# Two tiles' attention ahead of the weights, and a third tile in float32 products, in a fused attention and feed-forward kernel

## Chip, cores and metric

The kernel runs on one core of one Trainium2 chip. The metric is the device time of one execution in microseconds (us), and a lower time is better. The engines are called by their names in the profile: PE is the tensor engine, DVE the vector engine, ACT the scalar engine, POOL the GpSimd engine, and SP the engine that issues the transfers.

## What is computed

The reference is a decaying linear attention over 4 sequences of 768 positions with 8 heads of 64 features, followed by a two-layer feed-forward network with a squared ReLU:

```
for b in range(nb):
    intra = np.einsum('bhic,bhjc->bhij', qb, kb) * Dmask[None]
    intra = np.einsum('bhij,bhjd->bhid', intra, vb)
    inter = np.einsum('bhid,bhde->bhie', qb * lam_pow[None], kv_state)
    out[:, :, sl] = intra + inter
    kv_state = lam_block * kv_state + np.einsum('bhsd,bhse->bhde', kb * rev_pow, vb)
x = out as 3072 rows of 512
h = np.maximum(x @ w_in, 0.0)          # w_in 512 x 2048
return (h * h @ w_out)                 # w_out 2048 x 512
```

## The kernel before, in words

The 3072 rows are cut into 24 chunks of 128 positions, one for each sequence b and each of its six chunks c. Three chunks make a tile of 384 rows, so there are eight tiles (`TILES`). Tile 0 holds the chunks (0,0), (1,0), (2,0); tile 1 holds (3,0), (0,1), (0,2); tile 2 holds (0,3), (0,4), (0,5); every later tile holds further chunks of sequences 1 to 3. A chunk with c above 0 needs the state that the chunk before it in its sequence leaves behind.

**Attention.** Each chunk is worked in two units of four heads (q = 0 and 1), so a tile has six units. There are two forms. `unit_plain` multiplies float32 operands: scores (L312), the masked scores on DVE (L315), scaled values `vd` (L318), the state's update (L330, then `us` L340 and `diag` or `hold` L345 on DVE), the products with the old state and with the values (L357 and L360), and then `xr`, `xh` and `xl` (L363, L366, L367). `unit_split` cuts its operands into a high and a low part and multiplies these (L421, L441, L463, L464), which costs more work on ACT and DVE. The first `N_PLAIN` tiles take the plain form, the others the split form. The buffers of the plain form and of the weights (`pnt`, `diag0`, `diag1`, `st`, `m`) share their memory with those of the split form (`pkt`, `ab` and others): the split form starts when the last plain unit and the last weight are done.

**Weights.** The feed-forward network has 16 steps f. Each needs two halves of weights, 128 x 512 of the first layer (`wih`, `wil`) and 128 x 512 of the second (`woh`, `wol`). The weights arrive as 64-bit words. For each half ACT takes an absolute value (L271), DVE does four operations that turn the word into a float32 (L272, L274, L276, L278), ACT rounds the high part (L280), and DVE subtracts it for the low part (L281). There are three buffers `st` for arriving halves. After step 15 has been loaded the weights stay.

**Feed-forward step.** For one tile and one f, PE makes 12 products with 384 columns (L498) into `h`; ACT and DVE make `gh` and `gl` from it (for tiles 0 and 1 the ReLU, the square and the rounding are on ACT, later the square is repeated on DVE, L518); PE then makes six products with 512 columns (L504, L505) and three more (L507). Tiles have six PSUM banks and two `h` banks to share with the attention.

**Order.** All operations are listed with an engine, an expected length and a key. `Plan.order` goes through expected time and on each engine takes, among the operations that could start next, the one with the smallest key. The result is one fixed order for each engine; engines then wait only for data and buffers. The constants `FIRST`, `SLOW_STEP`, `LAG`, `SECOND` and `STEP` set the keys: tile 0's steps begin at `FIRST`, those of tile 1 sixteen steps later. Where `Plan.order` expects PE to be idle before `FILL_END`, it puts in a product of zeros (`filler`, L233), which writes into the second `h` bank. At the very start the table for the decay is turned by PE (`turned`, L245) after POOL has made the powers.

Of the kernel before, what the change touches and what calls it, by code (L numbers as in the profile page):

```python
# [19 lines left out]
P = 128  # L20
C = 128
# [18 lines left out]
TILES = [CHUNKS[j:j + NT] for j in range(0, B * NC_, NT)]  # L40
N_PLAIN = 2
PLAIN = [bc for t in TILES[:N_PLAIN] for bc in t]
# [18 lines left out]
class Plan:  # L61
# [16 lines left out]
    def order(self, pe_slow, fill):  # L78
# [9 lines left out]
        slots = {k: [(0.0, i) for i in range(n)] for k, n in self.slots.items()}  # L88
        done, early = [], sum(o.early is True for o in self.ops)
        while any(ready.values()):  # L90
# [25 lines left out]
            if o.eng == "PE" and t < fill:  # L116

                while free["PE"] + FILL < t:
                    done.append(Op("PE", FILL, 0, self.filler, [], [], [], 0, None))
                    done[-1].start, done[-1].end = free["PE"], free["PE"] + FILL  # L120
                    free["PE"] += FILL
            dur = o.dur * (2.0 if o.eng == "PE" and t < pe_slow else 1.0)
# [13 lines left out]
            for d in out.get(id(o), ()):  # L136
                need[id(d)] -= 1
                if not need[id(d)]:
                    ready[d.eng].append(d)
        assert sum(o.fn is not self.filler for o in done) == len(self.ops), "operations need each other"  # L140
        return done
# [12 lines left out]

FIRST, SLOW_STEP, LAG, SECOND, STEP, PE_SLOW, FILL_END, FILL = 18.0, 6.5, 16, 5.0, 4.8, 8.0, 24.0, 0.43

# [4 lines left out]
def kernel(ctx: ExitStack, tc: tile.TileContext, pn, pk, lamx, w, out):  # L161
# [69 lines left out]

    def filler():
        nc.tensor.matmul(tiles["h"][-1][:, 0:2 * P], zero[:, 0:P], zero[:, P:3 * P], start=True, stop=True)  # L233

# [8 lines left out]
    def turned():  # L243
# [6 lines left out]
        [o_pow], [wb], early=True)  # L250
    o = plan.op("PE", 0.9, 3, turned, [o], [wb, rps], early=True)
    o_rdec = plan.op("DVE", 0.6, 3, lambda: nc.vector.tensor_tensor(
# [42 lines left out]

    def unit_plain(b, c, q, x, col, key):

# [3 lines left out]
        def add(eng, dur, dk, fn, deps, bufs, name=None):  # L301
            o = plan.op(eng, dur, key + dk, fn, deps, bufs, early=True)
            return in_turn(name, o) if name else o

        load = add("SP", 1.7, -8, lambda: nc.sync.dma_start(out=at(t), in_=pn[PLAIN.index((b, c)), q]), [o_start], [t], "load")
        so = []
        for h in range(2):
            sc = Buf("bank")

            def scores(h=h, sc=sc):  # L310
                for n in range(2):
                    nc.tensor.matmul(at(sc)[:, n * C:n * C + C], at(t)[half(h), 0, n], at(t)[half(h), 1, n], start=True, stop=True)  # L312

            o = add("PE", 0.33, 0, scores, [load], [t, sc], f"sc{h}")
            so.append(add("DVE", 0.36, 0, lambda h=h, sc=sc: nc.vector.tensor_tensor(  # L315
                out=at(s1).rearrange("p (n h) i -> p n h i", h=2)[:, :, h], in0=at(sc)[:, 0:2 * C].rearrange("p (n i) -> p n i", n=2),
                in1=mask.unsqueeze(1).broadcast_to([P, 2, C]), op=ALU.mult), [o], [sc, s1], f"s1{h}"))
# [43 lines left out]

        o = add("PE", 1.25 if old else 0.8, 0.2, values, so + [o_vd] + ([old[1]] if old else []), [y, t, vd, s1] + ([old[0]] if old else []), "y")
        o = add("DVE", 0.35, 0.2, lambda: nc.vector.tensor_tensor(  # L363
# [7 lines left out]
    def unit_split(b, c, q, x, col, key, span):  # L371
# [83 lines left out]
        for h in range(2):  # L455
# [12 lines left out]

            o = add("PE", 0.48, 2, values, [ov2, op2, os2], [vv, pp, y, ss, ab], f"y{h}")
            o1 = add("ACT", 0.32, 2, lambda h=h, part=part: nc.scalar.copy(at(z)[:, h], part(1)), [o], [y, z], f"z{h}")  # L470
# [15 lines left out]

    last_mm = {}

    def ffn(ti, f, x, ready, wo, os_, key):
# [19 lines left out]
        o1 = plan.op("PE", 2.09, key, mm1, list(ready) + list(wo[0]), [x, h], [last_mm.get((ti, 1))])  # L509
        last_mm[ti, 1] = o1  # L510

        orr = plan.op("ACT", 0.45, key, lambda: nc.scalar.activation(at(g), at(h)[:, 0:N], AF.Relu), [o1], [h, g])  # L512
        if ti < N_PLAIN:
            og = plan.op("ACT", 0.45, key, lambda: nc.scalar.activation(at(g), at(g), AF.Square), [orr], [g])
            ogh = plan.op("ACT", 0.47, key, lambda: nc.scalar.copy(at(gh), at(g)), [og], [g, gh])  # L515
        else:
            ogh = plan.op("ACT", 0.47, key, lambda: nc.scalar.activation(at(gh), at(g), AF.Square), [orr], [g, gh])  # L517
            og = plan.op("DVE", 0.48, key, lambda: nc.vector.tensor_tensor(out=at(g), in0=at(g), in1=at(g), op=ALU.mult), [orr, ogh], [g])  # L518
# [34 lines left out]
    for ti, cs in enumerate(TILES):  # L553
# [3 lines left out]
        for j, (b, c) in enumerate(cs):  # L557
            for q in range(NQ):
                i = j * NQ + q
                if ti == 0:  # L560
                    ready += unit_plain(b, c, q, x, j * C, i * 1.5)
                elif ti < N_PLAIN:
                    ready += unit_plain(b, c, q, x, j * C, FIRST + 2 + i * SECOND)
                else:

                    f0 = 0.5 if ti > N_PLAIN else 2.0
                    ready += unit_split(b, c, q, x, j * C, begin[ti - 1] + (f0 + i / n * (13 - f0)) * per[ti - 1], 4.0)
# [59 lines left out]
```

## Time and profile before

| quantity | value |
|---|---|
| median of 3 runs | 660.7 us (660.07 to 660.84) |
| profiled execution | 660.94 us, its span 659.2 us |
| mean granted PE clock, share of full speed | 0.991 |
| PE busy | 641.5 us (97%), 3576 products |
| PE weight loads (PEld) | 576.3 us (87%) |
| DVE busy | 510.0 us (77%) |
| ACT busy | 364.7 us (55%) |
| POOL busy | 5.5 us (1%) |
| transfers | 58.30 MB, mean 88 GB/s |

The span is the time from the first to the last instruction of the profiled execution; 1.74 us of its time lie around the span. An engine is busy while one of its instructions runs. PE's products overlap, so a busy PE is not always a PE at its full rate: a product of 512 columns shows some 0.4 us, but the next one starts after 0.23 us. Where a duration counts below, it is therefore taken from one start to the next.

### The profile page before, as it was taken

The numbers are of one execution on the slowest core, as the hardware profiler recorded it, in microseconds if no ns is written. First come the engines' busy times: TensorE is split into PE (matmuls) and PEld (weight loads), VectorE is DVE, ScalarE is ACT, GpSimd is POOL, SyncE is SP. The second block draws the span as 40 slices with busy tenths as digits, with TensorE's granted clock in tenths as the row PEclk, the third lists the DMA queues.
The fourth block names the chain that finished last, engine by engine and source line by source line (L and its number), as shares of the span: only waits on it lengthen the run. The fifth ranks groups of instructions, "written<-read, shape, count | busy, mean of one in ns | idle before, by whom it ended". The sixth has DMA issues, their size and how long they took to land.

```text
span 659.2 us, 9528 instructions
## 1 busy us (share of the span) xinstructions
PE 641.5 (97%) x3576; PEld 576.3 (87%) x3576; DVE 510.0 (77%) x1150; ACT 364.7 (55%) x805; POOL 5.5 (1%) x15
## 2 busy tenths in 40 slices
PE   8869899999999999999999999999999999999997
PEld 7757798999989989899989999899998998999996
DVE  5979999978996889579995899848996698842222
ACT  2444576668884567456663565636665556532222
POOL 2000000000000000000000000000000000000000
PEclk9979899999999999999999999999999999999999
DMA  7733445622223112014111212220220221000001
GB/s 269 270 135 114 161 158 176 221 96 96 96 93 100 47 51 96 33 66 144 48 49 57 87 56 96 89 81 17 95 97 1 96 96 49 1 32 17 1 0 49
DMA packets 15167, 58.30 MB, mean 88 GB/s; under 512 B 1808, under 2 KB 1808, under 8 KB 15120
## 3 DMA queue, kind: packets, MB, share of 16 engines
q1 hardware_dynamic: 15120, 57.68, 25.5%
q8 instruction: 28, 0.46, 0.3%
q14 instruction: 19, 0.16, 0.1%
HBM read 51.39 MB, written 6.29 MB: 87 GB/s over the span
## 4 chain that ended last, share of the span: by engine, by line
PE 76%; DVE 19%; ACT 3%; DMA 1%; issue 1%; SPq 0%; ACTq 0%
PE h L498 33%; PE bank L507 12%; PE bank L504 11%; PE bank L505 11%; PE bank L464 2%; PE bank L463 2%; PE bank L421 2%; DVE gl L519 1%; DVE xr L476 1%; PE bank L441 1%; DVE ab L407 1%; DVE s L429 1%; PE h L233 1%; DVE ka L409 1%; DVE g L518 1%; DVE pp L433 1%
## 5 line engine op out<-in xcount | busy, mean ns | idle before, releaser
L504 PE MATMUL bank<-woh,gh 128*128 128x512 f32 x384 | 153.0, 398 | 2.1 <-ACT gh L515 2.1
L505 PE MATMUL bank<-wol,gh 128*128 128x512 f32 x384 | 152.2, 396 | 0.0
L512 ACT ACTIVATE g<-h 128x384 f32<-128x384 f32 x128 | 62.8, 491 | 132.1 <-PE h L498 131.5
L498 PE MATMUL h<-xh,wih 128*128 128x384 f32 x512 | 111.1, 339 | 5.1 <-ACT wih L280 5.1
L507 PE MATMUL bank<-woh,gl 128*128 128x512 f32 x384 | 112.8, 402 | 0.7
L518 DVE TENSOR_TENSOR g<-g 128x384 f32<-128x384 f32 x96 | 53.5, 557 | 77.3 <-ACT gh L517 76.8
L498 PE MATMUL h<-xh,wil 128*128 128x384 f32 x512 | 110.4, 338 | 0.0
L498 PE MATMUL h<-xl,wih 128*128 128x384 f32 x512 | 110.1, 337 | 0.0
L498 PEld LDWEIGHTS h<-xh,wih 128*128 128x128 f32 x512 | 90.6, 190 | 9.6 <-ACT wih L280 5.3
L498 PEld LDWEIGHTS h<-xh,wil 128*128 128x128 f32 x512 | 91.2, 189 | 0.0
L498 PEld LDWEIGHTS h<-xl,wih 128*128 128x128 f32 x512 | 91.0, 189 | 0.0
L507 PEld LDWEIGHTS bank<-woh,gl 128*128 128x128 f32 x384 | 70.1, 189 | 19.2 <-DVE gl L519 4.8
L504 PEld LDWEIGHTS bank<-woh,gh 128*128 128x128 f32 x384 | 72.5, 189 | 16.0 <-ACT gh L515 2.7
L505 PEld LDWEIGHTS bank<-wol,gh 128*128 128x128 f32 x384 | 72.7, 189 | 13.3
L519 DVE TENSOR_TENSOR gl<-g,gh 128x384 fp32r<-128x384 f32 x128 | 71.0, 556 | 8.7 <-ACT gh L515 4.5
L517 ACT ACTIVATE gh<-g 128x384 fp32r<-128x384 f32 x96 | 50.4, 525 | 2.5
L470 ACT COPY z<-bank 128x256 f32<-128x256 f32 x72 | 26.7, 371 | 38.2 <-PE bank L464 35.6
L471 DVE TENSOR_TENSOR z<-bank,z 128x256 f32<-128x256 f32 x72 | 30.0, 423 | 20.4 <-ACT z L470 18.8
L464 PE MATMUL bank<-pp,vv 128*128 128x256 f32 x144 | 35.8, 281 | 0.0
L463 PE MATMUL bank<-ab,ss 128*128 128x256 f32 x144 | 35.7, 281 | 0.0
L428 ACT COPY s<-bank 128x256 f32<-128x256 f32 x72 | 24.4, 373 | 17.7 <-PE bank L421 17.4
L476 DVE TENSOR_TENSOR xr<-z,zl 64x256 f32<-64x256 f32 x72 | 30.0, 417 | 2.5 <-ACT zl L472 1.0
(79 smaller groups left out, 801.3 us busy)
## 6 DMA issues: line engine op xcount, KB each, us to landing
pkt<-pk SPq DMA_DIRECT2D x36, 768.0 KB, 4.4
st<-w SPq DMA_DIRECT2D x32, 512.0 KB, 3.4
pnt<-pn SPq DMA_DIRECT2D x12, 512.0 KB, 4.7
out<-ob SPq DMA_DIRECT2D x23, 256.0 KB, 2.1
out<-z SPq DMA_DIRECT2D x1, 256.0 KB, 2.0
lam<-lamx SPq DMA_DIRECT2D x1, 6.0 KB, 1.6
```

The lines of the kernel that those rows point to most:

```text
L463: nc.tensor.matmul(y4[:, n], at(ss)[:, n, h].rearrange("p t d -> p (t d)"), at(ab)[:, i], start=n == 0, stop=False, skip_group_check=True)
L464: nc.tensor.matmul(y4[:, n], at(vv)[:, i].rearrange("p t d -> p (t d)"), at(pp)[:, i], start=False, stop=True, skip_group_check=True)
L471: zo.append(add("DVE", 0.36, 2, lambda h=h, part=part: nc.vector.tensor_tensor(out=at(z)[:, h], in0=part(0), in1=at(z)[:, h], op=ALU.add), ...
L476: nc.vector.tensor_tensor(out=at(xr)[half(h)], in0=at(z)[0:64, h], in1=at(zl)[:, h], op=ALU.add)
L498: nc.tensor.matmul(at(h)[:, 0:N], wt[:, cc, :], xt[:, cc, :], start=k == 0, stop=k == 3 * NCC - 1)
L504: nc.tensor.matmul(at(os_[j]), at(gh)[:, sl], woh[f], start=f == 0, stop=False)
L505: nc.tensor.matmul(at(os_[j]), at(gh)[:, sl], wol[f], start=False, stop=False)
L507: nc.tensor.matmul(at(os_[j]), at(gl)[:, sl], woh[f], start=False, stop=f == NF - 1)
L512: orr = plan.op("ACT", 0.45, key, lambda: nc.scalar.activation(at(g), at(h)[:, 0:N], AF.Relu), [o1], [h, g])
L517: ogh = plan.op("ACT", 0.47, key, lambda: nc.scalar.activation(at(gh), at(g), AF.Square), [orr], [g, gh])
L518: og = plan.op("DVE", 0.48, key, lambda: nc.vector.tensor_tensor(out=at(g), in0=at(g), in1=at(g), op=ALU.mult), [orr, ogh], [g])
L519: ogl = plan.op("DVE", 0.48, key, lambda: nc.vector.tensor_tensor(out=at(gl), in0=at(g), in1=at(gh), op=ALU.subtract), [og, ogh], [g, gh, gl])
```

## The change

The change sets `N_PLAIN` to 3, so tile 2 takes the plain form, and 30 split units remain of 36. The units of tile 2 are loaded no earlier than step 12 of tile 0 (`BEHIND`), and their values product takes the buffer of its tile's `x`. Tile 1's attention has keys from `BEGIN2` = 9 in steps of 1.5 instead of 20 in steps of 5, so it stands right behind that of tile 0 and ahead of nearly all weights; the order of the feed-forward steps of tile 0 and 1 follows from what can then start. The zero products write into a free bank instead of the second `h` bank, count as longer while PE is expected to be slow, may go on until 45, and stand at the start only until the first load is expected; the turning of the decay table waits for the first scores. ACT keeps the square for tiles 0 and 1 only (`ti < 2`, formerly `ti < N_PLAIN`), so tile 2's feed-forward steps are as before.

```
-N_PLAIN = 2
+N_PLAIN = 3
...
-                while free["PE"] + FILL < t:
-                    done.append(Op("PE", FILL, 0, self.filler, [], [], [], 0, None))
-                    done[-1].start, done[-1].end = free["PE"], free["PE"] + FILL
-                    free["PE"] += FILL
+                while free["PE"] + (long := FILL * (2.0 if free["PE"] < pe_slow else 1.0)) < t:
+                    bank = min(slots["bank"], default=(t, 0))
+                    if bank[0] > free["PE"]:
+                        break
+                    done.append(Op("PE", long, 0, lambda i=bank[1]: self.filler(i), [], [], [], 0, None))
+                    done[-1].start, done[-1].end = free["PE"], free["PE"] + long
+                    free["PE"] += long
+                    filled += 1
...
-FIRST, SLOW_STEP, LAG, SECOND, STEP, PE_SLOW, FILL_END, FILL = 18.0, 6.5, 16, 5.0, 4.8, 8.0, 24.0, 0.43
+FIRST, SLOW_STEP, LAG, BEGIN2, SECOND, STEP, PE_SLOW, FILL_END, FILL = 18.0, 6.5, 16, 9.0, 1.5, 4.8, 7.0, 45.0, 0.43
+
+BEHIND = 12
...
-    def filler():
-        nc.tensor.matmul(tiles["h"][-1][:, 0:2 * P], zero[:, 0:P], zero[:, P:3 * P], start=True, stop=True)
+    def filler(i):
+        nc.tensor.matmul(tiles["bank"][i][:, 0:2 * P], zero[:, 0:P], zero[:, P:3 * P], start=True, stop=True)
...
-        load = add("SP", 1.7, -8, lambda: nc.sync.dma_start(out=at(t), in_=pn[PLAIN.index((b, c)), q]), [o_start], [t], "load")
+        load = add("SP", 1.7, -8, lambda: nc.sync.dma_start(out=at(t), in_=pn[PLAIN.index((b, c)), q]), [o_start, behind], [t], "load")
...
+            if (b, c, q) == (0, 0, 0):
+                o_turned.after.append(o)
...
-        if ti < N_PLAIN:
+        if ti < 2:
...
+                elif ti == 1:
+                    ready += unit_plain(b, c, q, x, j * C, BEGIN2 + i * SECOND)
                 elif ti < N_PLAIN:
-                    ready += unit_plain(b, c, q, x, j * C, FIRST + 2 + i * SECOND)
+                    ready += unit_plain(b, c, q, x, j * C, begin[ti - 1] + (1 + i / n * 11) * per[ti - 1], steps[0, BEHIND])
```

What this does to the order shows at three places. In the rows, a name is that of the buffer written, then those read; lines of the changed kernel are six to eight higher (L233 is L239, L245 is L251, L312 is L318, L330 is L338, L360 is L368, L498 is L506, L504, L505 and L507 are L512, L513 and L515, L281 is L287).

The first place is PE at the very start, before:

```order
L233 MATMUL h_68<-ob_79 128x256 x11
L245 MATMUL bank_61<-g_77,m_184 128x128 x4
L312 MATMUL bank_62<-pnt_173 128x128 x2
L312 MATMUL bank_63<-pnt_173 128x128 x2
L312 MATMUL bank_64<-pnt_174 128x128 x2
L312 MATMUL bank_65<-pnt_174 128x128 x2
L330 MATMUL bank_66<-vd_90,pnt_173 64x64 x4
L360 MATMUL bank_61<-s_0_88,vd_90 64x128 x4
```

And now:

```order
L239 MATMUL bank_61<-ob_79 128x256 x5
L318 MATMUL bank_61<-pnt_173 128x128 x2
L318 MATMUL bank_62<-pnt_173 128x128 x2
L338 MATMUL bank_63<-vd_90,pnt_173 64x64 x4
L368 MATMUL bank_64<-s_0_88,vd_90 64x128 x4
L318 MATMUL bank_65<-pnt_174 128x128 x2
L318 MATMUL bank_66<-pnt_174 128x128 x2
L251 MATMUL bank_61<-g_77,m_184 128x128 x4
L368 MATMUL bank_62<-s_1_89,vd_91 64x128 x4
```

Six zero products have gone, and the first unit's scores, update and values product and the second unit's scores stand ahead of the turned table.

The second place is PE at its first feed-forward steps (`xh_95` is tile 0, `xh_97` is tile 1, `wih_106` is step 0, `wih_107` step 1), before:

```order
L498 MATMUL h_67<-xh_95,wih_106 128x384 x4
L498 MATMUL h_67<-xl_96,wih_106 128x384 x4
L498 MATMUL h_67<-xh_95,wil_122 128x384 x4
L330 MATMUL bank_63<-vd_90,pnt_175 64x64 x4
L312 MATMUL bank_61<-pnt_173 128x128 x2
L360 MATMUL bank_62<-s_0_88,vd_90 64x128 x4
L330 MATMUL bank_63<-vd_91,pnt_176 64x64 x4
L498 MATMUL h_68<-xh_95,wih_107 128x384 x4
L498 MATMUL h_68<-xl_96,wih_107 128x384 x4
L498 MATMUL h_68<-xh_95,wil_123 128x384 x4
L312 MATMUL bank_62<-pnt_174 128x128 x2
L498 MATMUL h_67<-xh_95,wih_108 128x384 x4
```

And now, from the last state update of tile 1 on:

```order
L338 MATMUL bank_64<-vd_91,pnt_176 64x64 x4
L239 MATMUL bank_62<-ob_79 128x256 x4
L506 MATMUL h_68<-xh_97,wih_106 128x384 x4
L506 MATMUL h_68<-xl_98,wih_106 128x384 x4
L506 MATMUL h_68<-xh_97,wil_122 128x384 x4
L515 MATMUL bank_61<-woh_138,gl_72 128x512
L515 MATMUL bank_65<-woh_138,gl_72 128x512
L515 MATMUL bank_66<-woh_138,gl_72 128x512
L506 MATMUL h_67<-xh_95,wih_107 128x384 x4
L506 MATMUL h_67<-xl_96,wih_107 128x384 x4
L506 MATMUL h_67<-xh_95,wil_123 128x384 x4
L512 MATMUL bank_62<-woh_138,gh_70 128x512
```

Before, PE went from step 0 of tile 0 to step 1 and step 2 of the same tile, with tile 1's attention between them; now step 0 of tile 1 stands between step 0 and step 1 of tile 0, and the attention of both is behind.

The third place is DVE around the low part of the third weight half (`wil_123` before and now), before, from row 52 on:

```order
L278 SCALAR_TENSOR_TENSOR m_186<-st_182,m_186 128x512
L274 TENSOR_SCALAR m_184<-m_184 128x512
L318 TENSOR_TENSOR vd_90<-pnt_175,wdec 128x256
L276 SCALAR_TENSOR_TENSOR m_184<-st_183,m_184 128x512
L281 TENSOR_TENSOR wol_154<-m_186,woh_138 128x512
L278 SCALAR_TENSOR_TENSOR m_184<-st_183,m_184 128x512
L315 TENSOR_TENSOR s_0_88<-bank_61,mask 128x2x128
L315 TENSOR_TENSOR s_0_88<-bank_62,mask 128x2x128
L345 TENSOR_TENSOR hold_84<-bank_63,lc 128x128
L318 TENSOR_TENSOR vd_91<-pnt_176,wdec 128x256
L281 TENSOR_TENSOR wil_123<-m_184,wih_107 128x512
```

And now, from row 95 on:

```order
L282 SCALAR_TENSOR_TENSOR m_184<-st_183,m_184 128x512
L371 TENSOR_TENSOR xr_94<-bank_63,rdec 128x256
L284 SCALAR_TENSOR_TENSOR m_184<-st_183,m_184 128x512
L375 TENSOR_TENSOR xl_98<-xr_94,xh_97 128x2x128
L527 TENSOR_TENSOR gl_72<-g_75,gh_69 128x384
L287 TENSOR_TENSOR wil_123<-m_184,wih_107 128x512
```

Before, the third half was done while tile 1's attention was at its first chunk; now it is done right behind the last `xl` of tile 1 (`xl_98`).

## Rows read from the trace of the kernel before

**Rows 1.** Stages (start:end, length; busy of PE, PEld, DVE, ACT, POOL; clock, DMA, GB/s)

```profile
20.00:30.00 10.00, 8.44 (x72) 6.40 (x72) 10.00 (x25) 4.72 (x10) 0.00 (x0) 1.00 0.67 224
30.00:40.00 10.00, 4.88 (x37) 4.37 (x37) 7.79 (x18) 5.41 (x10) 0.00 (x0) 0.82 0.56 211
80.00:90.00 10.00, 10.00 (x56) 9.55 (x55) 9.14 (x19) 8.77 (x19) 0.00 (x0) 1.00 0.46 158
```

**Rows 2.** Waits of PE (who waited for whom: us in total, times, longest)

```profile
PE h L498 <- ACT wih L280: 5.1, 1, 5.1
PE bank L441 <- DVE us L445: 1.4, 1, 1.4
```

**Rows 3.** Timeline of PE, step 2 of tile 0 (start, length, what, idle before)

```profile
38.86 1.65 PE L498 MATMUL h<-xh,wih 128*128 128x384 f32 x4 [5.12 <-ACT wih L280]
42.86 0.53 PE L504 MATMUL bank<-woh,gh 128*128 128x512 f32 x1
```

**Rows 4.** Timeline of PE from 76.97 us, steps end to end

```profile
76.97 1.01 PE L498 MATMUL h<-xh,wih 128*128 128x384 f32 x4
...
79.20 0.86 PE L498 MATMUL h<-xh,wih 128*128 128x384 f32 x4
...
85.44 0.39 PE L504 MATMUL bank<-woh,gh 128*128 128x512 f32 x1
...
86.84 0.86 PE L507 MATMUL bank<-woh,gl 128*128 128x512 f32 x3
87.54 0.86 PE L498 MATMUL h<-xh,wih 128*128 128x384 f32 x4
```

**Rows 5.** Stage of L498 alone, from 76.97 us to the end

```profile
76.97:659.20 582.23, 265.21 (x1464) 254.00 (x1463) 1.00 0.22 75
```

**Rows 6.** Chain that ended last, the same place in two successive tiles

```profile
264.21 0.96 PE bank L507 x3
...
341.86 0.97 PE bank L507 x3
```

**Rows 7.** Timeline of PE, last product

```profile
654.75 0.40 PE L507 MATMUL bank<-woh,gl 128*128 128x512 f32 x1
```

**Rows 8.** Timeline of PE, the zero products at the start

```profile
1.51 7.02 PE L233 MATMUL h<-ob 128*128 128x256 f32 x22 [1.51 <-DVE ob L217]
```

**Rows 9.** Timeline of DVE, the first unit's rows

```profile
9.46 0.69 DVE L252 TENSOR_TENSOR rdec<-bank,lam 128x512 f32<-128x512 f32 x1 [2.70 <-PE bank L245]
...
12.72 0.42 DVE L363 TENSOR_TENSOR xr<-bank,rdec 128x256 f32<-128x256 f32 x1
13.05 0.42 DVE L367 TENSOR_TENSOR xl<-xr,xh 128x256 fp32r<-128x256 f32 x1
...
14.39 0.58 DVE L345 TENSOR_TENSOR diag<-bank,lc 64x128 f32<-64x128 f32 x2
```

**Rows 10.** Timeline of DVE, two operations of a weight half

```profile
25.14 0.68 DVE L281 TENSOR_TENSOR wil<-m,wih 128x512 fp32r<-128x512 f32 x1
25.75 0.68 DVE L278 SCALAR_TENSOR_TENSOR m<-st,m 128x512 uint32<-128x512 uint32 x1
```

**Rows 11.** Stages of DVE alone (start:end, length; busy; clock, DMA, GB/s)

```profile
14.00:35.00 21.00, 20.92 (x56) 1.00 0.71 249
35.00:45.00 10.00, 6.69 (x16) 0.66 0.33 120
```

**Rows 12.** Stages of L281 alone, one for each weight half (the same columns)

```profile
77.00:100.00 23.00, 4.81 (x7) 0.99 0.49 163
100.00:122.00 22.00, 5.00 (x8) 1.00 0.53 172
```

**Rows 13.** Timeline of PE, one plain unit with an old state

```profile
12.15 0.72 PE L312 MATMUL bank<-pnt 64*128 64x128 f32 x8
...
47.98 0.60 PE L357 MATMUL bank<-pnt,diag 128*128 128x128 f32 x4
...
49.00 0.40 PE L330 MATMUL bank<-vd,pnt 128*64 128x64 f32 x8
49.33 0.50 PE L504 MATMUL bank<-woh,gh 128*128 128x512 f32 x1
```

More of the change, by code (lines that the diff above doesn't have):

```diff
@@ L88, in order @@
         slots = {k: [(0.0, i) for i in range(n)] for k, n in self.slots.items()}
-        done, early = [], sum(o.early is True for o in self.ops)
+        done, filled, early = [], 0, sum(o.early is True for o in self.ops)
         while any(ready.values()):
@@ L139, in order @@
                     ready[d.eng].append(d)
-        assert sum(o.fn is not self.filler for o in done) == len(self.ops), "operations need each other"
+        assert len(done) - filled == len(self.ops), "operations need each other"
         return done
@@ L250 @@
         [o_pow], [wb], early=True)
-    o = plan.op("PE", 0.9, 3, turned, [o], [wb, rps], early=True)
+    o_turned = o = plan.op("PE", 0.9, 3, turned, [o], [wb, rps], early=True)
     o_rdec = plan.op("DVE", 0.6, 3, lambda: nc.vector.tensor_tensor(
@@ L294, with unit_plain @@
     half = lambda h: slice(h * 64, h * 64 + 64)
-    def unit_plain(b, c, q, x, col, key):
+    def unit_plain(b, c, q, x, col, key, behind=None):
         prs = slice(2 * q, 2 * q + 2)
@@ L360, in values @@
                     nc.tensor.matmul(o_[half(h), n], at(vd)[:, 2 * n + h], at(s1)[:, 2 * n + h], start=not old, stop=True, skip_group_check=True)
-        o = add("PE", 1.25 if old else 0.8, 0.2, values, so + [o_vd] + ([old[1]] if old else []), [y, t, vd, s1] + ([old[0]] if old else []), "y")
+        o = add("PE", 1.25 if old else 0.8, 0.2, values, so + [o_vd] + ([old[1]] if old else []), [y, t, vd, s1, x] + ([old[0]] if old else []), "y")
         o = add("DVE", 0.35, 0.2, lambda: nc.vector.tensor_tensor(
@@ L467, in part @@
                 return at(y).rearrange("p (n t i) -> p n t i", n=2, t=2)[:, :, i]
-            o = add("PE", 0.48, 2, values, [ov2, op2, os2], [vv, pp, y, ss, ab], f"y{h}")
+            o = add("PE", 0.48, 2, values, [ov2, op2, os2], [vv, pp, y, ss, ab, x], f"y{h}")
             o1 = add("ACT", 0.32, 2, lambda h=h, part=part: nc.scalar.copy(at(z)[:, h], part(1)), [o], [y, z], f"z{h}")
@@ L484, in unit_split @@
         return [oh, ol]
-    last_mm = {}
+    last_mm, steps = {}, {}
     def ffn(ti, f, x, ready, wo, os_, key):
@@ L509, in ffn @@
         o1 = plan.op("PE", 2.09, key, mm1, list(ready) + list(wo[0]), [x, h], [last_mm.get((ti, 1))])
-        last_mm[ti, 1] = o1
+        last_mm[ti, 1] = steps[ti, f] = o1
         orr = plan.op("ACT", 0.45, key, lambda: nc.scalar.activation(at(g), at(h)[:, 0:N], AF.Relu), [o1], [h, g])
-        if ti < N_PLAIN:
+        if ti < 2:
             og = plan.op("ACT", 0.45, key, lambda: nc.scalar.activation(at(g), at(g), AF.Square), [orr], [g])
@@ L561 @@
                     ready += unit_plain(b, c, q, x, j * C, i * 1.5)
+                elif ti == 1:
+                    ready += unit_plain(b, c, q, x, j * C, BEGIN2 + i * SECOND)
                 elif ti < N_PLAIN:
-                    ready += unit_plain(b, c, q, x, j * C, FIRST + 2 + i * SECOND)
+                    ready += unit_plain(b, c, q, x, j * C, begin[ti - 1] + (1 + i / n * 11) * per[ti - 1], steps[0, BEHIND])
                 else:
-                    f0 = 0.5 if ti > N_PLAIN else 2.0
+                    f0 = 0.5 if ti > 2 else 2.0
                     ready += unit_split(b, c, q, x, j * C, begin[ti - 1] + (f0 + i / n * (13 - f0)) * per[ti - 1], 4.0)
```

## Prediction

> **What bounds the kernel now.** I first read the stages for the place where PE stops losing time. From 20 to 30 us PE shows 8.44 us of 10 and DVE 10.00; from 30 to 40 us PE shows 4.88 us at a granted clock of 0.82; at 80 to 90 us it is full at clock 1.00 [rows 1]. The waits name the largest loss: 5.1 us in which PE waits for ACT's `wih` of step 2 [rows 2, 3]. After 76.97 us one wait of 1.4 us is all that stands there [rows 2]. So the reader should see two regimes: a start in which DVE and the weights set the pace, and from 76.97 us on a PE that is simply full.
>
> The full regime can be rebuilt from starts. Three times twelve products of L498 take 85.44 - 79.20 = 6.24 us, 2.08 a step; the six of L504 and L505 take 1.40, the three of L507 0.70 [rows 4]. A feed-forward step is 4.18 us. From 76.97 us on there are 1464 records of L498, 122 steps of twelve [rows 5], so 6 of 128 are done by then. Two successive tiles lie 77.65 us apart [rows 6]; less 16 x 4.18 = 66.9 that leaves 10.8 us for the split attention of one tile. The last product starts at 654.75 us [rows 7], 4.45 before the end. Together 122 x 4.18 + 6 x 10.8 + 4.45 = 579.2 us, against 659.2 - 76.97 = 582.2. The missing 3.0 hold the wait of 1.4 and 1.6 of small gaps.
>
> So the time is the moment from which PE is full, plus the work that is left then. By 76.97 us PE has done only 6 steps (25 us) and the attention of twelve units (some 21 us, below).
>
> **The change, part by part.** *When PE becomes full.* Before, DVE has to interleave tile 1's attention with the weights, and PE can only follow tile 0 as its weights come. Now both attentions come first, and each weight pair that follows feeds two steps, one of each tile: 8.36 us of PE work. PE can be full as soon as `xl` of tile 1 is written (row 98 of DVE's order), and DVE decides when that is.
>
> DVE's first part: eleven zero products took 7.02 us, 22 records [rows 8], so five take 3.2 us, or 4 if the first are the slow ones, and the first scores run at about 5.2 us instead of 9.4. DVE's idle 2.70 us ahead of `rdec` [rows 9] goes mostly; but the first two units now pass PE one after the other (scores 0.35, values 0.7, the turned table 1.0, values 0.7, each handed over to DVE). I put the scaling of the second unit at 10.7 us, where it was 12.72 [rows 9], done at 11.0. It can't be earlier than 9.5 (DVE's own rows laid end to end) nor, by the rows now ahead of it, later than 13.05.
>
> From there to the last `xl` the new order has 85 DVE instructions: 57 of 0.33 us (the pace from 12.72 to 13.05), six short state rows of at most 0.33, seven pairs for states of 0.6 [rows 9], and eight weight operations of 0.61 [rows 10]. That is 18.8 + 2.0 + 4.2 + 4.9 = 29.9 us, end to end 40.9. Idle time on top: DVE lost 0.1 of 21 us between 14 and 35 us, and 3.3 of 10 between 35 and 45 [rows 11]. By the first rate it is nothing, by the second 10 us. The work is that of the first stretch (attention of independent chunks with a few weight rows between), except that tile 1's chunks (0,1) and (0,2) depend on each other; I take 2.1, so PE is full from **43.0 us**.
>
> Up to then PE has made the twelve products of tile 0's step 0 and its first six (2.08 + 1.40), 0.83 of a step; 127.17 are left: 531.6 us.
>
> *The weights behind it.* DVE finished 15 halves in the 45 us from 77 to 122 [rows 12], with the `gl` rows of both tiles between, 6.0 us a pair. In the new order PE has 14 steps of tile 0 and 7 of tile 1 between step 1 and step 15 of tile 0: 21 x 4.18 / 14 = 6.27 us a pair. So the weights stay ahead, but by 0.27 us a pair only, and the first three or four pairs have hardly a reserve. I add 1.5 us of PE waits there; the bounds are nothing and the 5.1 of [rows 2]. ACT was 8.77 of 10 busy in that regime [rows 1] and its load is the same.
>
> *Loads.* Tile 1's six loads stand on SP's queue ahead of the second and later weight pairs, each behind a buffer that PE and DVE must release. A load is 512 KB; at 224 GB/s with the DMA engines 0.67 busy [rows 1] a full rate is 334 GB/s, 1.6 us a load, against some 3 us that DVE takes for one unit. They are covered by DVE; without that cover they would cost what the idle bound above holds.
>
> *Tile 2 in plain products.* A plain unit with an old state costs PE 0.72 for scores, 1.02 for the values (47.98 to 49.00) and 0.33 for the update [rows 13]; two of six have no update. That is 6 x 2.07 - 0.66 = 11.8 us instead of 10.8: a loss of 1.0 us, always on PE's path. DVE and ACT work falls, but lies under PE either way. The units of sequence 0 are a chain, and 8 steps of tile 1 (33 us of PE) lie between their first scores and tile 2's first step; DVE needs some 17 us for them. The change also removes the place of the 1.4 us wait, at the end of tile 1. For the new chain and the later opening of the split form I put 1.0 us back, with bounds 0 and 5.
>
> *Zero products.* Six go at the start, and later ones need a free bank. Their cost was idle time, so taking them costs nothing unless PE's clock falls. After the 5.12 us wait twelve products took 42.86 - 38.86 = 4.00 instead of 2.08 us at a lower clock [rows 3]: 1.9 us for one fall. With no wait of that length in the new start I price none. The Trainium skill (TensorE: Matmul & The Clock Gate, "HAM oscillation") says that an engine that idles between bursts goes back to half clock and starts each burst slow; by that rule the waiting attention phase could run at 1.2 GHz as a whole, which is the third rival. The stage of 20 to 30 us, at 8.44 busy and clock 1.00 [rows 1], does not bear it out for this density.
>
> **Sum.** 43.0 + 531.6 + 5 x 10.8 + 11.8 + 4.45 + small gaps 1.6 + 1.5 + 1.0 = 649.0 us of span. With 1.74 around it that is 650.7 of one execution; the profiled one (660.94) lay 0.24 above the median, so **650.5 us**, 10.2 less than before.
>
> **Rivals.**
> First, DVE idles more than I take, or the weights come late. If DVE idles in the new start as from 35 to 45 us, PE is full only at some 49 us, and 656.5 results; with one wait of 5.1 us in the weights it is 660, no change. For it speak the small reserve of the first pairs and a fixed order that can't give way; against it the 0.1 of 21 us. A sharper form: if a pair takes DVE 7.0 us instead of 6.0, PE loses 14 x 0.73 = 10.2 us, and the gain is gone.
>
> Second, everything goes smoothly: no added idle on DVE (40.9) and no waits take 2.1 + 2.5 off, 646; with no small gaps either 644.3.
>
> Third, the other side: the clock. Until 43 us PE has 20.6 us of attention (four units of 2.07, eight of 1.54 without an old state), 3.5 of step 0, 1 of the table and about 6 of zero products, 31 us of work in the 38 from 5 on, so 7 us are free. Where x us of that work runs at 1.2 GHz, x - 7 are lost: from x = 17 on the change is no gain, and with all 31 the time is 650.5 + 24 = 674. For it speaks that this phase waits on DVE at every unit; against it that the same products ran at clock 1.00 from 20 to 30 us, less densely than they stand now, with a few zero products between as now.
>
> Fourth, tile 2's chain is late: the slack is 33 - 17 = 16 us, so it costs something only from a delay of 16 us, and takes the gain from 26. Nothing in the trace speaks for that.
>
> **How the numbers follow.** Forecast with its own range 646 to 655: 0.70. First rival, 655 to 661: 0.14. Second, below 646: 0.07. Third, 661 to 674: 0.07. Fourth: 0.02. The range 646 to 657 leaves out the second, the third, the fourth and half of the first: it holds about 0.77, so I set it at 645.5 to 657.5. What a measurement of this kernel can tell from no change is 0.2%, 1.3 us. Faster: 0.70 + 0.07 and most of the first, 0.88; the same 0.04; slower 0.08.
>
> **What would show it.** In the changed kernel PE should show no wait above 2 us after some 43 us, tile 1's first twelve products should start at 41 to 46 us, and the clock should be 1.00 in every stage from 45 us on. DVE should be full from 11 to 125 us. The distance of two late tiles should still be 77.65 us, with the whole gain already there where tile 3 begins. I am wrong if L506 of tile 0 waits for `wih` or `wil` again and again between 45 and 130 us, if the clock is below 1 between 10 and 40, or if tile 2's first product waits for its `xl`.

## The result and the profile after

| quantity | before | after |
|---|---|---|
| median, same chip | 660.38 us (657.92 to 660.84, 4 runs) | 651.77 us (651.0 to 652.86, 4 runs) |
| span of the profiled execution | 659.2 us | 649.8 us |
| mean granted PE clock | 0.991 | 0.997 |
| PE busy | 641.5 us (97%) | 640.6 us (99%) |
| DVE busy | 510.0 us (77%) | 483.3 us (74%) |
| ACT busy | 364.7 us (55%) | 341.2 us (53%) |

The ratio is 0.9878, 95% interval 0.985 to 0.9907: the kernel is 1.2% faster. On the two chips of the experiments the kernel before had medians of 658.03 and 658.26 us over 17 runs each, from 655.81 to 662.24, and on the second, beside the last two kernels below, 657.05 over ten. The changed kernel ran again on the first of these chips: 652.31 us in six runs, from 651.55 to 652.56. So the gain was 8.6 us beside the first result and 5.7 in the repetition, and the changed kernel varies less.

The times of the kernel before go with its mean granted clock: on those two chips it took 655.80 to 656.34 us in the ten runs with a clock of 0.997, and 661.30 to 662.24 in the six with 0.989. The changed kernel took 651.55 to 652.86 us in its nine runs at 0.996 and 0.997. At like clock the gain is therefore some 4 us, and the rest is lower clock, of which the kernel before has more in most of its runs.

The stages of all engines after (start:end, length; busy; clock, DMA, GB/s), which answer to [rows 1], with the stretch of the weights and that of tile 2's plain attention at the end:

```profile
20.00:30.00 10.00, 8.17 (x79) 7.09 (x78) 9.88 (x30) 2.52 (x5) 0.00 (x0) 0.83 0.72 261
30.00:40.00 10.00, 10.00 (x99) 7.96 (x99) 8.57 (x25) 4.25 (x9) 0.00 (x0) 1.00 0.16 52
40.00:50.00 10.00, 10.00 (x61) 9.33 (x58) 9.78 (x24) 5.92 (x12) 0.00 (x0) 1.00 0.33 100
...
41.89:130.00 88.11, 88.11 (x447) 79.99 (x446) 87.02 (x175) 64.96 (x123) 1.05 (x2) 1.00 0.56 185
...
130.54:170.69 40.15, 40.15 (x276) 33.02 (x275) 20.25 (x54) 10.96 (x24) 0.00 (x0) 1.00 0.22 81
```

PE has no gap from 30 us on, where it was busy for 4.88 us of 10 before; up to 41.89 us some 3 us of that are zero products. All of PE's waits in the execution (us, times, longest) are these, against [rows 2]:

```profile
PE bank L239 <- DVE ob L223: 1.5, 1, 1.5
PE bank L318 <- DMA pnt<-pn: 1.4, 1, 1.4
PE bank L338 <- DVE vd L326: 0.6, 2, 0.4
PE bank L512 <- ACT gh L523: 0.4, 1, 0.4
```

The 5.1 us for `wih` have gone, and nothing of that size has come in their place. The timeline of PE shows where tile 1's first step begins, and the end of the span:

```profile
41.89 1.05 PE L506 MATMUL h<-xh,wih 128*128 128x384 f32 x4
...
44.17 0.86 PE L515 MATMUL bank<-woh,gl 128*128 128x512 f32 x3
44.87 0.86 PE L506 MATMUL h<-xh,wih 128*128 128x384 f32 x4
...
48.34 0.86 PE L506 MATMUL h<-xh,wih 128*128 128x384 f32 x4
...
645.28 0.40 PE L515 MATMUL bank<-woh,gl 128*128 128x512 f32 x1
```

The first-layer products alone, from that moment to the end, answer to [rows 5]: 1524 records, 127 steps of twelve.

```profile
41.89:649.80 607.91, 276.65 (x1524) 264.40 (x1524) 1.00 0.23 79
```

And the chain that ended last has the place of [rows 6] in these moments:

```profile
254.41 0.96 PE bank L515 x3
332.07 0.97 PE bank L515 x3
```

Before it stood at 264.21 and 341.86: between the two traced executions 9.80 and 9.79 us of gain are there already, and the last product still has 654.75 - 645.28 = 9.47 of them [rows 7]. Their distance is 77.66 us, as before.

### The profile page after: what moved, and what is told of

The parts are those of the page before. It is cut to its first block, busy times and chain, and to the rows that moved or that the text cites. A ratio compares the mean times of both kernels' runs of the same rounds, so it can differ in the third digit from the quotient of the medians.

```text
span 649.8 us, 9509 instructions
## 1 busy us (share of the span) xinstructions
PE 640.6 (99%) x3636; PEld 573.2 (88%) x3636; DVE 483.3 (74%) x1090; ACT 341.2 (53%) x739; POOL 5.5 (1%) x15
## 4 chain that ended last, share of the span: by engine, by line
PE 83%; DVE 13%; DMA 2%; ACT 1%; issue 1%; SPq 0%; DVEq 0%; ACTq 0%
PE h L506 35%; PE bank L515 13%; PE bank L512 12%; PE bank L513 12%; PE bank L472 2%; PE bank L471 2%; PE bank L429 2%; PE bank L239 1%; PE bank L318 1%; PE bank L449 1%; DVE xr L484 1%; PE bank L368 1%; DVE gl L527 1%; DMA pkt<-pk 1%; DVE g L526 1%; DVE s L437 1%
## 5 line engine op out<-in xcount | busy, mean ns | idle before, releaser
L512 PE MATMUL bank<-woh,gh 128*128 128x512 f32 x384 | 152.3, 397 | 0.4 <-ACT gh L523 0.4
L513 PE MATMUL bank<-wol,gh 128*128 128x512 f32 x384 | 151.7, 395 | 0.0
L515 PE MATMUL bank<-woh,gl 128*128 128x512 f32 x384 | 112.0, 400 | 0.7
L506 PE MATMUL h<-xh,wih 128*128 128x384 f32 x512 | 111.2, 339 | 0.0
L506 PE MATMUL h<-xl,wih 128*128 128x384 f32 x512 | 109.8, 336 | 0.0
L506 PE MATMUL h<-xh,wil 128*128 128x384 f32 x512 | 109.8, 336 | 0.0
L506 PEld LDWEIGHTS h<-xh,wih 128*128 128x128 f32 x512 | 90.6, 189 | 4.5
L506 PEld LDWEIGHTS h<-xl,wih 128*128 128x128 f32 x512 | 90.9, 189 | 0.0
L506 PEld LDWEIGHTS h<-xh,wil 128*128 128x128 f32 x512 | 90.6, 188 | 0.0
L515 PEld LDWEIGHTS bank<-woh,gl 128*128 128x128 f32 x384 | 70.1, 188 | 19.8 <-DVE gl L527 4.6
L512 PEld LDWEIGHTS bank<-woh,gh 128*128 128x128 f32 x384 | 72.2, 188 | 14.0 <-ACT gh L523 0.7
L513 PEld LDWEIGHTS bank<-wol,gh 128*128 128x128 f32 x384 | 72.2, 188 | 13.5 <-DVE wol L287 0.3
L478 ACT COPY z<-bank 128x256 f32<-128x256 f32 x60 | 22.3, 372 | 38.4 <-PE bank L472 35.8
L479 DVE TENSOR_TENSOR z<-bank,z 128x256 f32<-128x256 f32 x60 | 25.1, 424 | 14.2 <-ACT z L478 12.7
L472 PE MATMUL bank<-pp,vv 128*128 128x256 f32 x120 | 29.8, 281 | 0.0
L471 PE MATMUL bank<-ab,ss 128*128 128x256 f32 x120 | 29.8, 281 | 0.0
L436 ACT COPY s<-bank 128x256 f32<-128x256 f32 x60 | 20.0, 373 | 14.5 <-PE bank L429 14.3
L484 DVE TENSOR_TENSOR xr<-z,zl 64x256 f32<-64x256 f32 x60 | 25.0, 417 | 2.0 <-ACT zl L480 1.0
```

Of the source, the lines that this page charges most:

```text
L471: nc.tensor.matmul(y4[:, n], at(ss)[:, n, h].rearrange("p t d -> p (t d)"), at(ab)[:, i], start=n == 0, stop=False, skip_group_check=True)
L472: nc.tensor.matmul(y4[:, n], at(vv)[:, i].rearrange("p t d -> p (t d)"), at(pp)[:, i], start=False, stop=True, skip_group_check=True)
L479: zo.append(add("DVE", 0.36, 2, lambda h=h, part=part: nc.vector.tensor_tensor(out=at(z)[:, h], in0=part(0), in1=at(z)[:, h], op=ALU.add), ...
L484: nc.vector.tensor_tensor(out=at(xr)[half(h)], in0=at(z)[0:64, h], in1=at(zl)[:, h], op=ALU.add)
L506: nc.tensor.matmul(at(h)[:, 0:N], wt[:, cc, :], xt[:, cc, :], start=k == 0, stop=k == 3 * NCC - 1)
L512: nc.tensor.matmul(at(os_[j]), at(gh)[:, sl], woh[f], start=f == 0, stop=False)
```

## The experiments

Each kernel below was run beside the kernel before on its chip. A ratio is to those runs.

**The changed kernel again**, as a yardstick for the three kernels after it, with no edit.

> The changed kernel again, as the yardstick of this chip. Every theory: 651 to 652 us, a span near 649.8 us, tile 1's first product of L506 near 41.9 us.

Measured: 652.31 us (651.55 to 652.56), ratio 0.9915 (0.9892 to 0.9937). The place in the chain is at 254.50 us.

**The third tile split again.**

```
-N_PLAIN = 3
+N_PLAIN = 2
```

> The changed kernel with tile 2 back in the split form (36 split units). My theory: the whole gain comes from PE being full from 41.9 us, and the plain form of tile 2 costs PE (six units took 15.0 us there, split ones take 10.8). So the start is the same and the time is 4 us lower, 647 to 648.5 us, if the split units of tile 2 hide behind tile 1's last steps. Rival: the split form can only open when the last weight is done, near 130 us, and its work on ACT and DVE then makes PE wait at the end of tile 1 (1.4 us there before); with waits of 4 us or more the time is 652 us or above, and the plain form was needed for the gain.

Measured: 655.78 us (654.26 to 656.59), ratio 0.9957 (0.9936 to 0.9977), 3.5 above the changed kernel on the same chip, as the rival has it and not the theory. Tile 1's first step began at 40.41 us, 1.48 earlier than in the changed kernel, but the place in the chain came at 258.16.

The earlier start has its own cause, and it prices something that the changed kernel lost. Up to tile 1's first step PE's order is the same but for one zero product. What differs is the clock: 1.00 from 20 to 30 us here (PE's stage, first line), 0.83 in the changed kernel. One row of DVE shows the effect, here (second line) and in the changed kernel (third line):

```profile
20.00:30.00 10.00, 8.17 (x96) 1.00 0.77 263
...
30.67 0.42 DVE L371 TENSOR_TENSOR xr<-bank,rdec 128x256 f32<-128x256 f32 x1
...
31.52 0.42 DVE L371 TENSOR_TENSOR xr<-bank,rdec 128x256 f32<-128x256 f32 x1 [1.12 <-PE bank L368]
```

The DVE row before it starts 0.23 us later here (30.22 against 29.99), and from three rows behind it up to 39.5 us DVE is 1.05 us ahead: the lower clock cost the changed kernel's start 1.3 us.

PE's four waits at the end of tile 1 in the kernel with the split third tile, from its table of waits, and the last two stages in which they lie:

```profile
PE h L506 <- ACT xh L489: 3.8, 1, 3.8
...
PE bank L472 <- DVE pp L441: 1.2, 1, 1.2
PE bank L515 <- DVE gl L527: 0.9, 1, 0.9
...
PE bank L429 <- DVE ab L415: 0.7, 1, 0.7
```

```profile
180.00:190.00 10.00, 4.88 (x32) 3.94 (x30) 9.72 (x24) 7.82 (x20) 0.00 (x0) 0.94 0.44 155
190.00:200.00 10.00, 9.42 (x36) 8.84 (x37) 7.37 (x17) 3.06 (x6) 0.00 (x0) 0.72 0.01 4
```

The waits at the end of tile 1 (178 to 191 us) sum to 6.6 us, and the clock of 0.72 from 190 to 200 us adds up to 2.8. DVE is 9.72 of 10 busy there: the split form can open only when the last weight is done (DVE's last row for it starts at 127.38 us, the first split cast at 127.63), and it then has six units to finish before tile 1 ends. My first theory, that the plain third tile only costs, fell. It costs PE more, but it is free of that gate; without it 658.03 - 655.78 = 2.3 us of the gain are left on this chip, of 5.7.

**The third tile plain, without the early attention**: the kernel before with `N_PLAIN = 3` and what that needs.

```
-N_PLAIN = 2
+N_PLAIN = 3
...
-        if ti < N_PLAIN:
+        if ti < 2:
...
+                elif ti < N_PLAIN:
+                    ready += unit_plain(b, c, q, x, j * C, begin[ti - 1] + (1 + i / n * 11) * per[ti - 1], steps[0, BEHIND])
```

> The kernel before with only tile 2 in the plain form; tile 1's attention and the zero products stay as they were. My theory: the start is the old one, PE full near 77 us; the plain units cost PE 1 to 4 us more and remove the wait of 1.4 us, so 660 to 663.5 us. Rival: the plain form of tile 2, with less work for ACT and DVE, brings a good part of the gain; then 656 us or less.

Measured: 662.18 us (661.81 to 663.08), ratio 1.0068 (1.0045 to 1.0091). Alone it is a loss of 4 us against the 658.03 of that chip, as expected. All the rest of the change without it gives 2.3, both together 5.7: the two parts need each other.

**No zero products.**

```
-FIRST, SLOW_STEP, LAG, BEGIN2, SECOND, STEP, PE_SLOW, FILL_END, FILL = 18.0, 6.5, 16, 9.0, 1.5, 4.8, 7.0, 45.0, 0.43
+FIRST, SLOW_STEP, LAG, BEGIN2, SECOND, STEP, PE_SLOW, FILL_END, FILL = 18.0, 6.5, 16, 9.0, 1.5, 4.8, 7.0, 0.0, 0.43
```

> The changed kernel without any zero product. Theory: the attention products themselves keep PE's clock up for most of the start, and the zero products only cover the first microseconds and the gaps of one to two microseconds; without them the clock is below 1 for some more of the first 45 us, but DVE sets the pace there, so tile 1's first step starts at 42 to 45 us: 652 to 655 us. Rival (the clock rival of the prediction): the start falls to 1.2 GHz as a whole, PE sets the pace, tile 1's first step starts after 52 us: above 661 us.

Measured: 651.15 us (650.21 to 651.92), ratio 0.9885 (0.9852 to 0.9917), no slower than the changed kernel with its medians of 651.77 and 652.31 (it did not run on this chip) and faster than the 652 to 655 that I expected. Three stages of its start:

```profile
10.00:20.00 10.00, 9.26 (x118) 6.82 (x116) 9.27 (x28) 3.13 (x7) 0.00 (x0) 1.00 0.82 300
20.00:30.00 10.00, 8.17 (x86) 7.03 (x83) 9.94 (x30) 2.42 (x5) 0.00 (x0) 0.85 0.81 272
30.00:40.00 10.00, 8.89 (x86) 6.91 (x86) 8.96 (x26) 4.25 (x9) 0.00 (x0) 0.98 0.15 54
```

The clock is about that with zero products (0.83 from 20 to 30 us there), so the zero products are worth nothing here. The third rival has no ground: the attention phase does not fall to 1.2 GHz as a whole with PE 8.17 to 9.26 of 10 busy. The Trainium skill (TensorE: Matmul & The Clock Gate, "HAM oscillation") tells of bursts that start slow behind waits. The traces agree at single places only: the 0.85 above from 20 to 30 us, the 0.83 of the changed kernel there, and one place in the next kernel.

**The clamp of each weight half on DVE twice** (32 times 0.33 us, 10.7 us more on DVE).

```
         o = add("DVE", 0.35, lambda: nc.vector.tensor_scalar(
             out=at(m), in0=at(m), scalar1=W_MIN, scalar2=W_MAX, op0=ALU.max, op1=ALU.min), [o], [m])
+        o = add("DVE", 0.35, lambda: nc.vector.tensor_scalar(
+            out=at(m), in0=at(m), scalar1=W_MIN, scalar2=W_MAX, op0=ALU.max, op1=ALU.min), [o], [m])
```

> The changed kernel with one DVE operation of each weight half done twice (same result): 0.335 us a half, 10.7 us in all, a weight pair some 6.7 us of DVE instead of 6.0, more than the 6.27 us in which PE passes a step of tile 0 and half a step of tile 1. Sharper form of the first rival: PE waits 0.4 us at each of 14 pairs, 657 us. My theory now, since the changed kernel showed no wait of PE at all between 42 and 130 us: steps of tile 1 stand ready to fill in, the order is made with the longer operation in it, and PE loses little: 651.8 to 653.5 us.

Measured: 655.27 us (653.64 to 656.04), ratio 0.9948 (0.9931 to 0.9964), 3.0 to 3.5 us above the changed kernel's two medians and above the 651.8 to 653.5 expected; the traced execution took 654.33, which is 2.8 above the traced one of the changed kernel. DVE now finished the last twelve halves in 139.77 - 99.45 = 40.3 us, 6.7 a pair (after: ten in 130.80 - 100.62 = 30.2, 6.0 a pair), and still PE had no wait between 50 and 140 us. The loss lies at one place, here PE's timeline (its L508, L514 and L517 are L506, L512 and L515 of the changed kernel):

```profile
43.15 0.86 PE L508 MATMUL h<-xh,wil 128*128 128x384 f32 x4
46.07 0.50 PE L514 MATMUL bank<-woh,gh 128*128 128x512 f32 x1 [2.06 <-ACT gh L525]
...
48.27 1.48 PE L508 MATMUL h<-xh,wih 128*128 128x384 f32 x4
...
51.21 0.86 PE L517 MATMUL bank<-woh,gl 128*128 128x512 f32 x3
```

The weights of step 1 are late here: their low part starts on DVE at 45.98 us instead of 42.90. PE has nothing left but the second-layer products of tile 1's step 0, which the order now puts ahead of step 1, and it waits 2.06 us for their `gh`; products at a lower clock follow (0.84 from 40 to 50 us). At 51.21 us PE has done what the changed kernel has done at 48.34, 2.9 us later, which agrees with the 2.8 us between the two traces. In its sharper form the first rival would let PE wait 0.4 us (6.7 - 6.27) at each of 14 pairs; that is refuted, since there is no wait between 50 and 140 us: where pairs come later the order gives PE steps of tile 1 in between, whose weights are there.

**The scaling `vd` of the first two tiles twice** (4.0 us more on DVE in the start).

```
+        for again in range(2 if behind is None else 1):
+            o_vd = add("DVE", 0.35, 0, lambda: nc.vector.tensor_tensor(
...
```

> The changed kernel with one DVE operation of each plain unit of tiles 0 and 1 done twice (same result): 12 times 0.335 us, 4.0 us of DVE ahead of tile 1's last row. Theory (DVE sets when PE is full): tile 1's first step starts 4 us later, near 46 us, and the time is 655 to 656 us. Rival (PE or the loads set it): the start moves by less than 1 us and the time stays at 652 us.

**Their scores twice** (7.8 us more on PE in the start).

```
+                for _ in range(2 if behind is None else 1):
+                    for n in range(2):
+                        nc.tensor.matmul(at(sc)[:, n * C:n * C + C], at(t)[half(h), 0, n], at(t)[half(h), 1, n], start=True, stop=True)
...
+            o = add("PE", 0.66 if behind is None else 0.33, 0, scores, [load], [t, sc], f"sc{h}")
```

> The changed kernel with the score products of the twelve plain units of tiles 0 and 1 done twice (same result): 12 times 0.65 us, 7.8 us of PE in the start. Theory (DVE sets when PE is full, PE has about 7 us free there and about 6 us of zero products): tile 1's first step starts at most 2 us later, 651.8 to 654 us. Rival (PE sets it): 7.8 us later, near 659.5 us.

Measured: 653.92 us (653.14 to 654.33), ratio 0.992 (0.9891 to 0.9949), and 654.38 us (654.17 to 655.36), ratio 0.9937 (0.9912 to 0.9963). The last `xl` of tile 1 in DVE's timeline, first of the changed kernel, then of the one with `vd` twice, then of the one with the scores twice:

```profile
42.09 0.42 DVE L375 TENSOR_TENSOR xl<-xr,xh 128x256 fp32r<-128x256 f32 x1
```

```profile
44.99 0.42 DVE L376 TENSOR_TENSOR xl<-xr,xh 128x256 fp32r<-128x256 f32 x1
```

```profile
45.01 0.42 DVE L376 TENSOR_TENSOR xl<-xr,xh 128x256 fp32r<-128x256 f32 x1
```

Both come 2.9 us later. But both ran at a clock of 1.00 in every stage from 10 to 50 us, and the changed kernel's start had lost 1.3 us to its lower clock (the third tile split, above); without that its row would stand at some 40.8 us, and both shifts are 4.2. So the 4.0 us on DVE come through whole, and of the 7.8 us on PE 4.2 do. DVE sets the start in the changed kernel, as the theory says, but PE has only some 3.6 us free there, not the 7 that I had worked out: with the scores twice PE is itself 10.00 of 10 busy in each stage from 10 to 40 us. Both expectations missed in part: 655 to 656 us for the first, and at most 2 us of shift for the second.

**Both score halves of a plain unit together.** In the changed kernel each half is an operation of its own, and the order may put other work between them.

```
-            def scores(h=h, sc=sc):
+        def scores():
+            for h, sc in enumerate(scs):
...
+        o = add("PE", 0.66, 0, scores, [load], [t] + scs, "sc")
```

> The changed kernel with the scores of a plain unit's two halves as one step of the order, so that they always stand next to each other on PE. In the changed kernel two of tile 2's six units have their halves apart, and each half alone took 0.64 us where the two together take 0.65. Theory: those four lone halves cost 1.3 us, and the start, which DVE sets, does not change: 650.3 to 650.8 us where the changed kernel has 651.8. Rival: the lone halves fill time in which PE would wait for DVE; then no change, 651.5 to 652.

Measured: 650.21 us (650.02 to 653.42), ratio 0.9892 (0.9866 to 0.9918). It gained, but not only in tile 2: tile 1's first step came at 40.20 us, 1.69 earlier than in the changed kernel. From 25 to 35 us PE has no wait for a `pnt` load, its clock is 1.00 instead of 0.83, and DVE is 9.72 of 10 busy instead of 8.60. Of the 1.69 us some 1.3 are that clock, by the price found with the third tile split, where the halves stood as in the changed kernel. At 174.21 us there was a new wait of PE of 2.54 us.

**The same kernel, with ACT's first split casts later.** The new wait should come from ACT's queue, so this kernel changes that queue alone: the casts for tile 3's first two units come behind the rounding of tile 1's step 13.

```
+        first = [rounded[1, 13]] if SPLIT.index((b, c)) == 0 else []
...
-        oa = add("ACT", 0.57, 0, lambda: nc.scalar.copy(at(ab)[:, :, 0], q4()), [load], [t, ab], "ab")
+        oa = add("ACT", 0.57, 0, lambda: nc.scalar.copy(at(ab)[:, :, 0], q4()), [load] + first, [t, ab], "ab")
...
-            ogh = plan.op("ACT", 0.47, key, lambda: nc.scalar.copy(at(gh), at(g)), [og], [g, gh])
+            ogh = rounded[ti, f] = plan.op("ACT", 0.47, key, lambda: nc.scalar.copy(at(gh), at(g)), [og], [g, gh])
```

> The same kernel as in the run in which both score halves stand together, as the yardstick beside the later casts on the same chip: 650.2 us within 0.7, with the wait of about 2.5 us for gh near 174 us again. If that wait changes by more than 1 us from run to run, its size was chance.

> As the kernel in which both score halves of a plain unit stand together, and in addition ACT's seven casts for the first two split units (tile 3) stand behind the ReLU, square and rounding of tile 1's steps 12 and 13 instead of ahead of them. Theory (the 2.5 us in which PE waits at 174.21 us for ACT's gh come from these casts, which wait 3.03 us for their load while the feed-forward rows queue behind them): the wait goes to below 0.5 us and PE is full from there; the place in tile 2 where the chain reads 253.23 us comes at some 251, and the time is 2.0 to 2.5 us below that kernel, near 648. Rival (the wait only moves: the split units of tile 3 start 3.5 us later and are late at the end of tile 2, as they were at the end of tile 1 in the kernel whose third tile is split): a new PE wait of 1 to 4 us on xh, pp or a bank appears between 190 and 245 us, and the time is no better than 650.

Measured on one chip: 649.72 us (649.41 to 652.05) without, ratio 0.9892 (0.9865 to 0.992), and **647.1 us** (646.57 to 647.96) with the later casts, ratio 0.9847 (0.9821 to 0.9872). ACT's timeline without them:

```profile
169.18 0.62 ACT L414 CAST ab<-pkt 128x512 fp32r<-128x512 f32 x1 [2.94 <-DMA pkt<-pk]
169.71 0.61 ACT L416 CAST ka<-pkt 128x512 fp32r<-128x512 f32 x1
...
171.85 0.61 ACT L405 CAST ss<-hold 64x128 fp32r<-64x128 f32 x2
172.49 0.49 ACT L520 ACTIVATE g<-h 128x384 f32<-128x384 f32 x1
173.01 0.52 ACT L522 ACTIVATE g<-g 128x384 f32<-128x384 f32 x1
173.56 0.51 ACT L523 CAST gh<-g 128x384 fp32r<-128x384 f32 x1
```

PE's timeline of that kernel:

```profile
174.13 0.50 PE L512 MATMUL bank<-woh,gh 128*128 128x512 f32 x1 [2.35 <-ACT gh L523]
```

And ACT's with the later casts (lines one or two higher):

```profile
169.44 0.49 ACT L521 ACTIVATE g<-h 128x384 f32<-128x384 f32 x1 [3.50 <-PE h L507]
169.96 0.53 ACT L523 ACTIVATE g<-g 128x384 f32<-128x384 f32 x1
170.52 0.51 ACT L524 CAST gh<-g 128x384 fp32r<-128x384 f32 x1
...
173.03 0.62 ACT L415 CAST ab<-pkt 128x512 fp32r<-128x512 f32 x1
```

ACT had stood at a cast whose load was not there, and the ReLU queued behind six casts; with the casts behind it the ReLU runs 3.05 us earlier and PE's wait is gone, as the theory has it. The chain's place is at 250.24 us instead of 253.14, 2.9 earlier, and no new wait appears between 190 and 245 us. This is the best version that was run. The split form opens the same way in the changed kernel (its cast waits 3.07 us at 170.44), but there PE arrives later and loses only 0.4 us.

## Why the prediction was right

**When PE becomes full**: 43.0 us forecast, 41.89 measured, inside 41 to 46, with the last `xl` at 42.09. The scaling of the second unit (10.7 forecast, done at 11.0) ended at about 11.15. From there the counting of rows carried it: DVE's idle time was 1.6 of 28 us from 14 to 42, against the 2.1 that I took, and the bound of 10 us did not occur. That the idle time came out so near was luck. I took it for the dependence of tile 1's chunks, and 1.12 us of it is the one wait for PE behind the lower clock, which I had priced at nothing; nor were the loads all covered, since PE waited 1.45 us for one. Less the 1.3 us of the lower clock, by my estimate, the start would have been near 40.6 us, close to the second rival's 40.9. That DVE alone decides this moment was too simple: 7.8 us more on PE moved it as well.

**The weights behind it**: 1.5 us forecast, nothing measured. From 41.89 to 130 us PE is 88.11 of 88.11 busy, DVE 87.02. I called the reserve thin at 0.27 us a pair. The doubled clamp shows why that measure was wrong: the second tile is a reserve of sixteen steps, and a later pair moves a step of tile 1 forward instead of stopping PE. Only the first pair behind step 0 has no such cover, and there the doubled clamp cost 2.9 us.

**Tile 2 in plain products**: 11.8 us forecast, 15.05 measured. This is the term that I mis-sized. The stretch from 130.54 to 170.69 holds five times twelve products (10.4), seven sets of L512 and L513 (9.8) and seven of L515 (4.9) besides the six units: 40.15 - 25.1 = 15.05. Three places of PE's timeline in it:

```profile
138.31 0.72 PE L318 MATMUL bank<-pnt 64*128 64x128 f32 x8
138.96 0.96 PE L515 MATMUL bank<-woh,gl 128*128 128x512 f32 x3
139.86 0.45 PE L338 MATMUL bank<-vd,pnt 128*64 128x64 f32 x8
140.24 0.71 PE L365 MATMUL bank<-pnt,diag 128*128 128x128 f32 x4
...
141.47 0.71 PE L318 MATMUL bank<-pnt 64*128 64x128 f32 x4
142.11 0.62 PE L506 MATMUL h<-xh,wih 128*128 128x384 f32 x2
...
144.39 0.71 PE L318 MATMUL bank<-pnt 64*128 64x128 f32 x4
145.03 0.45 PE L338 MATMUL bank<-vd,pnt 128*64 128x64 f32 x8
```

The eight records of both halves together take 138.96 - 138.31 = 0.65 us, the four of one half alone 142.11 - 141.47 = 0.64. I had priced a unit's scores at 0.72, the length of a row with both halves [rows 13], but in two of six units the halves stand apart: 4 x 0.65 + 2 x 1.28 = 5.2 us, not 4.3. The values products take 1.12 us, or 1.23 behind an update (140.24 to 141.47), and the update 0.38 where I took 1.02 and 0.33: 1.0 more. The remaining 1.4 lies in the feed-forward products between the units. From start to start the five sets of twelve take 10.9 us there, the seven of L512 and L513 10.2 and the seven of L515 5.4, together 26.5 instead of 25.1; the set from 138.96 to 139.86, next to a unit's products, takes 0.90 instead of 0.70. I had priced the units alone and nothing for their neighbours.

With the halves together and the casts late the same sets and units stand between these two lines of PE:

```profile
128.66 0.86 PE L507 MATMUL h<-xh,wih 128*128 128x384 f32 x4
...
167.16 0.86 PE L507 MATMUL h<-xh,wih 128*128 128x384 f32 x4
```

That is 38.5 us, so the units cost 13.4 instead of 15.05. Of the 1.65 us saved, 1.26 is what four lone halves cost more than two pairs (2 x 1.28 - 2 x 0.65); the rest goes with the order of other work, which moved a little as well.

The Trainium skill (TensorE: Matmul & The Clock Gate, "Part 3: Packing small matmuls — row/col tiling") says that products on different row groups of the array run side by side. The trace agrees for two float32 halves of 64 rows that stand next to each other, at 0.65 us for eight records.

**Chain and opening of tile 3**: 1.0 us forecast, the 0.4 us wait for `gh` measured. That the change removes the crowding at the end of tile 1 is shown by the kernel with a split third tile, where it returned with 6.6 us of waits: this part of the change is worth more than the prediction said, and it is no saving in products but a gate that is opened.

**Sum.** 649.0 us of span was forecast, 649.8 measured: -1.1 for the start, -1.5 for the weights, +3.25 for tile 2 and -0.6 for the opening give 649.05. The other 0.75 is less than two executions of one kernel differ by: behind the chain's place at 254 us alone the same work took 395.0 us before, 395.4 after and 396.3 in the repeated run. The mechanism held, a PE that is full from a moment that DVE sets, and the work left then; that the time came out to 0.8 us was luck, since errors of -3.2 and +3.25 cancelled. The gain did not come out so well: 10.2 us forecast, 8.6 and 5.7 measured. I took it from a median of three runs of the kernel before (660.07 to 660.84 us), and these, like the traced one with its mean clock of 0.991, were among its slower ones.

**The rivals.** The first did not occur, and its sharper form is refuted. Of the second the missing waits behind the start occurred and about half of its earlier start (41.89 between 43.0 and 40.9), without its time, since tile 2 took the gain. The third fell with the kernel without zero products, though the clock did fall once, to 0.83 between 20 and 30 us, where I had said that a clock below 1 before 40 us would show me wrong: a wait of 1.45 us for a `pnt` load at 24.62 lay ahead of it, and twelve products from 26.91 took 3.37 us instead of 2.08. DVE then waited 1.12 us for PE at 31.52. So by my own sign it was wrong to price the clock at nothing: the fall cost 1.3 us within the 41.89, by the kernel with the split third tile. The fourth did not occur.

## What to carry to other kernels

When one engine is full, find the moment from which it is full and count what is left; what a change gives is the shift of that moment, and a second independent stream of work behind it is a larger reserve than the pace of the supply suggests. A stage that is gated by shared memory (here the split form behind the last weight) crowds what comes behind the gate; a dearer form that is free of the gate can pay. In a fixed order for an in-order engine, an early row that waits for a load holds up every ready row behind it, so put it behind the rows that a full engine waits for.

## What was not expected of the hardware

Two score products on the two row halves of PE cost together what one costs alone (0.65 and 0.64 us in the records above), so it is the neighbourhood in the order that halves their price. A lower clock followed short waits: behind 1.45 us of waiting at 24.62 us in the changed kernel and 2.06 us at 46.07 us with the clamp twice the granted clock of the stage was 0.83 and 0.84. Yet waits of like length did not always bring it: with the clamp twice PE waited 1.27 us at 24.61 us for a `pnt` load too and the stages from 20 to 40 us kept 1.00, and after the wait of 2.35 us at 174.13 us, which came after a long full stretch, the stage of 170 to 180 us kept 1.00. What tells these apart was not settled.
